# A freshly searched order for all engines, a stricter rule for the last product, and 88 in place of 64 opening identity products, in a fused attention and feed-forward kernel

## The chip, the cores and the metric

The kernel runs on one core of one Trainium2 chip. A core has a matrix engine (TensorE, PE in the profile), a vector engine (VectorE, DVE), an activation engine (ScalarE, ACT), a general engine (GpSimd, POOL) and a synchronisation engine (SyncE, SP) that here issues most of the DMA transfers. Each engine works through its own queue in the order in which the program gave it the instructions. The metric is device time in microseconds (us), the median over runs. Six runs of the kernel before gave 435.27 to 436.93 us, median 435.7.

## The reference

Attention with normalised queries and keys, followed by a two-layer product with a gate between. All matrices are float32 at the boundary.

```python
q, k, v: (8, 12, 448, 64)      # batch, heads, sequence, head width
q_n = q / (norm(q) + 1e-06);  k_n = k / (norm(k) + 1e-06)
scores = q_n @ k_n.T / tau                       # tau = 0.1
attn = softmax(scores)                           # with 1e-09 in the denominator
x = (attn @ v), heads side by side               # (3584, 768)
h = x @ w_in                                     # w_in (768, 2048)
g = h * sigmoid(1.702 * h)
out = g @ w_out                                  # w_out (2048, 768)
```

## The kernel before, in words

**Tiles and names.** The heads are handled in 24 quads `y` of four heads, three quads to a batch element, so that quads 0 to 2 are batch 0, 12 to 14 batch 4, and so on. A quad has two pairs `x` of heads. For each quad these operations exist; the line in brackets is the one under which the profile shows them.

- `load`: q and k (L268 for quad 0, in halves of which SP's and ACT's queue take one each, L276 for the others) and v (L287) come in by DMA. All but ACT's two halves take turns in a fixed sequence.
- `sq` (L309, L310): q and k are squared, 128 x 896 numbers at a time. `red` (L318) sums the squares on DVE.
- the inverse norms: for batch 0 by logarithm, exponential and reciprocal (`root`, `inv`, L330 to L341), later by steps of an iteration on DVE (`norm`, L349 to L377).
- `scale` (L409 for k, in three pieces; L410 for q): multiplication by the inverse norm, into 16 bit.
- `tp`, `qkT` (L434, L445): quads 0 to 4 are transposed on TensorE and copied; later ones by a transposing DMA.
- `kL` (L461): a small copy of the last 64 keys.
- `s` (L483, L512): score products into PSUM; `exp` (L521): the exponential on ACT, which frees the score buffer. There are two score buffers.
- `cast` (L421, L425, L426): v into 16 bit. `at` (L550, L561): the attention product. `nx` (L573, L589): division by the row sum on DVE. `turn`, `x` (L599 to L632): the transposition of the result.

Then follows the feed-forward part. `mm1` (L643, and in halves for batch 0 L674) multiplies by w_in; `th` (L653) is the tanh on ACT and `g` (L660, L686) the gate on DVE; `mm2` (L699) multiplies by w_out in four parts of four products each; `ost` (L712 on DVE, L713 on ACT) copies half a tile of the output out of PSUM, and `st` (L718) stores it. The work of later quads lies beside the feed-forward work of earlier ones.

**The order.** Every operation is added to a plan with an engine, an estimated duration, a due time, its predecessors and the buffers that it takes and frees. While the program is built, `order` plays this through: whenever an engine is free, it takes the ready operation with the earliest due time. The result is the fixed sequence of instructions in each engine's queue; on the chip nothing is rearranged. `tune` first moves each due time by the letter that belongs to it in the string DUES (steps of 0.25 us, the letter K for no move) and chooses an engine for each of 254 operations that have a choice, by the digit in the string ENGINES (0 for the engine given first, 1 and 2 for the alternatives). The turns of the loads are numbered by the due times as they were before the letters are applied. The strings were found by a search outside of the program.

**Identity products.** Ahead of the whole plan, at L989, TensorE multiplies the identity by itself WARM_UP times; nobody uses the result. In the first 48 us of the plan, further identity products (L474) fill gaps that the plan foresees on TensorE; their number follows from the length of the gap.

**The last product's predecessors.** `mm2` of part p reads the gated tiles 4p to 4p + 3. The plan names the gate of the last of these four (for batch 0, whose gates handle two tiles at a time, that of tiles 4p + 2 and 4p + 3) as its predecessor.

Of the kernel before, what the change touches and what calls it, by code (L numbers as in the profile page):

```python
# [24 lines left out]
DMA_ENGINES = 16  # L25
PACKET_US = {256: 0.033, 1024: 0.072, 1536: 0.064, 1792: 0.078, 3072: 0.135, 4096: 0.178}
MOE_FROM, MOE_LAG = 8, 9
FILL_TO, WARM_UP, FILL_US = 48, 64, 0.032
STEPS = "#$%&()*+,-./0123456789:;<=>?@ABCDEFGHIJKLMNOPQRSTUVWXYZ[]^_abcdefghijklmnopqrst"
DUES = (  # L30
    "tGmtOMKLKKMLTPUKXIKtBKATDQKOUH;K:LK#?K>L@]M8MKCE2e>MIKKbHg;BCJKFkIhKKTBLLUKRKrLMFJ]PAK;cgKYKHjpTqCKKXSNt"
    "MKWgSFgKbtNiIT]C7K3KK5ZLtKGQKTcEGPKbFKJ/KtGetI7KAPKLLE?KCK#&@HNM%KMKKLEZk<JJW=KbTKKK@AEPKItMYKtWtETDsG9H"
    "fKSdCWssJLKRRK:KcGK[LHHGGXHt>JAKKcFtJBOOoNKPPMVa_MHN)ttsKTK@KLK@IKaKTiKKCOCInKoYKJKNHnLKRtCBKMLtth[tLtKK"
    "WtttSsJtZPLRKJLHKLKNJKJIKDtKbM@ttQKfWLe@JtGMK;JtKt9KHRKKtKcSL#nsPPmiIqEptsYqKUtS=TMaG]1K1nLrs9[t(tLKeKn["
    "NLSKKVK?KKKtHnf]#[@XMKLBJKc[ICt^3TQ-LN6JHL?<Ka#DtC)KKKIKO(SLPT+IKHSK>KKH#LCKU<KS@HKEI]?KW#GLKK?pLKWKmt3K"
    "tKLK,IJKIKHFL(eGdJZKYRMEFQJCAPOtQM#K/hMKNdNNJ2LLEKPKKKNLKmJKN_T<KOs<t#GHODR?9LU;KOKMT2M9f4KN2#n*1sKT&LKK"
    "Z3<KII3JKJPtKLIKGQStEG@cJsJ3tVKKKKEFtj9.MINAEKJH<KH@KQOE9KJIJ1JAGNHKGG:k$<K)OSBK#LKKRHFL?PLhKgKKfpX004;K"
    "6:tKhKkIK[tNHEKk8L1-KKSWPQI1B1@-L$FQ%dDK#Hp42K;NK(KJFI@&BKUXKKMPRMKG#0%##C1#_K-0JGZYhK#KLcNK8dfKM#J9HpKa"
    "NGJ#Z54KKG)&-PJCF(@KGI7#KCNIG#MkLC<KJKJGV.10oKI7J#M[jM#9LJGIOKKbCMtKK]I]K8ESILPPKG#1&W%UK,JJHQU,+FMKKBJT"
    "MH#K-YhRGd1KJHGEKMPKUGW_aMVKKO=er8JWRLNB@KKASG=Kf=AKUHp^KYHkX=QLJJRiJ>Kbs^UiKKKWIOK637KK$H=*KPKKMJKJP.4F"  # L40
    "KD<RDKD6KK/KD3$J=AH*6G?=G4aF*.K:[KBLLJR+HH#OtHPJ@LLFME@8LVKIN#JKDS)N#UhKL#JNLK*HIBKO;KHt1HTDRKD2@UE7KKMK"
    "MM&K9DIILC:?F?FK&:BWJ?HD]LbLK$5BCN/EY-L#QUMZJHMQ6KLMNJICGFEGO#BKNeohKTKVKGTBK3KLKLJ0ASONK7LL@OA3JKNVKKSO"
    "IRtNOKHOEIKJOXQHIENKJJtQO9K5S,MJSFTBORO@$QKE1DBLKI/HKKSFOKOKISHOKLJFgNDbHKKPNEKL[>PDLKBSDKnKK[2ZLKNTtKsQ"
    "K]IEKVKY*KDKUKUNPJaOb_:SK7ZUMU=tOKHKK3#PJI;o_LK][MKLKKCI/HJa@K#;W+KK-tMXKKLtdG%KIqJEDTYRL,EhKJrKMQ5%HI[P"
    "K#JMHWpNGDPSMINFB^ONJ_&K#K>#iaMj[RJMVLWKOEL_1KCHRTKKRPLFG*#KWPG%LICtI+@FKE9KKBPBK?K?W1=YFKKSMKQWK#?fIsMn"
    "F[JF##KM.JK,4X#KPH)NDIQKQW67AK*KWFLV0EN5ORHM;KIJ/#PKBGQOJK0KPKHU[K+KFKKKQJMJ#Iec3b#KI;7LOH[KK6#KKD4OLBGK"
    "ftKttL"
)
ENGINES = (
    "00200100100101020000000011110010100000111020100110100001110101120000001112000002010000001010100110000211"  # L50
    "10100010100101000000010000000100001000220000001000100000100220100000000000210111010001122101001000000010"
    "0000100000010110100000100001100011000110100010"
)


def packets(n, nbytes):

    one = PACKET_US[nbytes]
    return n * one / DMA_ENGINES, one
# [132 lines left out]
def kernel(  # L192
# [12 lines left out]
    B, H, S, D = q.shape  # L205
    NTOK, DM = out.shape
    DFF = moe_w_in.shape[1]
    P = 112
    C = S // 64
    HP = H // 2  # L210
# [536 lines left out]
    def due_of(y):  # L747
        return 2 * y if y < ND else 4 * y
# [12 lines left out]
    for y in range(NDUO):  # L761
        b, s, grp = y // ND, due_of(y), group_of[y]
# [3 lines left out]
        for ti, nm in ((1, "k"), (0, "q")):  # L766
            pl = on_pool(y, ti)
            n = 0.55 if y == 0 else 1
            for j in (0, 1) if y == 0 else (None,):
# [4 lines left out]
                else:  # L774
# [25 lines left out]
        for ti in (1, 0):  # L800
# [3 lines left out]
                after=[scales[ti]] + [("scale", 1, y)] * (not ti and y > 1), takes=[("qks", 2 if y < 2 else 4 * ti)],  # L804
# [5 lines left out]
        for g in range(2):  # L810
            x = 2 * y + g
            add(("cast", x), "POOL", 1.0, s + (g if first else 2 * g) - 0.5, partial(cast_v, x),
                after=[("load", "v", y, half) for half in range(2)] + [("cast", x - 1)] * g + [("at", x - NV, 1)] * (x >= NV),
                takes=[("vt", 1)], frees=[("v", g)], alts=[("DVE", 0.86)])
        if y < TURNED:
            for ti in (1, 0):
                add(("tp", ti, y), "PE", 0.45, s - 3, partial(turn_qk, y, ti),
                    after=[("scale", ti, y)] + [("tp", 1, y)] * (not ti and y > 1), takes=[("mm", 1), ("qkT", ti)], frees=[("qks", 2)])
# [5 lines left out]
        else:  # L824
            add(("qkT", y), "SP", 3.6, s - 3, partial(dma_turn, y),
                after=[("scale", 0, y), ("scale", 1, y)], takes=[("qkT", 1)], frees=[("qks", 4)],
# [26 lines left out]
        for g in range(2):  # L853
            x = 2 * y + g
            for h in range(2):
# [3 lines left out]
                else:  # L859
# [7 lines left out]
                    after=[("at", x, h)] + [("nx", 2 * y, 0)] * (not turned and g + h > 0) + [("nx", x, 0)] * (whole and h),  # L867
# [21 lines left out]
    def product(name, us, emit, after, takes, frees, tail):  # L889
        moe.append((name, us, emit, after, takes, frees, tail))  # L890

    for b in range(B):
        b2 = b // 2
        units = [(h, m) for h in range(2) for m in range(0, KT2, 2)] if b == 0 else [(b, m) for m in range(KT2)]
        prev = last1
        for u in units:
            key = u if b else u + ("h",)
            m, half = u[1], not b
            after = [prev] if prev else []
            if half and m == 0:  # L900
                after += [("x", x, u[0]) for x in range(HP)]
            elif m == 0:
                after += [("x", x, h) for x in range(b * HP, (b + 1) * HP) for h in range(2) if h and (x < 2 * TX or x % 2)]
            if b == 0:
                after += [("w_in", m // 8, j) for j in range(2)]
            last = u == units[-1]
            prev = ("mm1",) + key
            product(prev, 1.134, partial(mm1_h if half else mm1, *u), after, [("mm", 1)], [("x", HP * last)],
                [("th", "ACT", 0.55, partial(tanh, *key), [("th", 1)], []),
                 ("g", "DVE", 0.62, partial(gate_h if half else gate, *u),  # L910
                  [("g", int(b % 2 == 0 and u == units[0]))], [("th", 1), ("mm", 1)])])
        last1 = prev
        tiles = (0, 1, 2) if b % 2 == 0 else (3, 4, 5, 6)
        for t in tiles:
            for n in range(2):
                for part in range(4):
                    if b:
                        after = [("g", b, 4 * part + 3)]
                    else:
                        after = [("g", h, 4 * part + 2, "h") for h in range(1 + (t > 0))]  # L920
                    after.append(("w_out", part // 2))
                    after += [last2] if last2 else []
                    last2 = ("mm2", b2, t, n, part)
                    last = t == tiles[-1] and n == 1 and part == 3
                    tail = []
                    if part == 3:
                        split = b == B - 1 and t == tiles[-1]
                        tail = [("ost", "ACT", 0.5, partial(halve, b2, t, n), [("ost", 1 - n)], [("mm", 1)])]
                        if n == 1 or split:
                            cols = slice(NW * n, NW * (n + 1)) if split else slice(0, DM)  # L930
                            for i in range(2):
                                queue = "ACT" if split and i else "SP"
                                tail.append((("st", i), queue, packets(64, 4 * (cols.stop - cols.start)),
                                    partial(store, b2, t, i, cols, nc.scalar if queue == "ACT" else nc.sync), i,
                                    [("ost", int(n == 1 and i == 1))]))
                    product(("mm2", b2, t, n, part), 0.652, partial(mm2, b2, t, n, part), after,
                        [("mm", int(part == 0))], [("g", int(last and b % 2))], tail)

    total, done = sum(u[1] for u in moe), 0.0
    for name, us, emit, after, takes, frees, tail in moe:  # L940
        b, part = divmod(B * done / total, 1)
# [82 lines left out]
```

## Time and profile before

| what | value |
|---|---|
| median of six runs | 435.7 us (435.27 to 436.93) |
| the profiled execution, its own time | 437.96 us |
| the profiled execution, span from first to last instruction | 436.2 us |
| mean granted TensorE clock | 0.992 |
| chain that ended last, by engine | PE 80%, DMA 10%, ACT 3%, DVE 3%, POOL 2% |
| exponentials, L521 on ACT | 171, mean 904 ns, 147.5 us busy |
| L699 on PE | 896 products, 157.1 us busy |
| L643 on PE | 672 products, 136.6 us busy |
| opening products, L989 | 64, 5.8 us busy |
| fill products, L474 | 229, 5.8 + 2.8 us busy |

A row of the profile's groups gives the line, the engine, the operation, what it writes and reads with shapes, and a count; then the busy time and the mean of one in ns; then the idle time of the engine just before them, with what ended it. Busy shares of the engines are averages over stages, and a wait matters only where it holds up the chain that ends last. The clock row gives TensorE's granted clock in tenths of full speed over 40 slices. In a list of windows each engine has its busy time and, in brackets, its count of instructions, in the sequence PE, weight loads, DVE, ACT, POOL; then come the granted clock, the DMA share and GB/s. In a timeline a line starts with the start and the duration in us, and ends, in square brackets, with the engine's idle time before and what ended it.

### The profile page before, as it was taken

How to read it: one execution, taken by the hardware profiler on the slowest of the kernel's cores; microseconds unless marked ns; L12 is line 12 of the kernel's file. 1: busy time of each engine (PE TensorE's matmuls, PEld its weight loads, DVE VectorE, ACT ScalarE, POOL GpSimd, SP SyncE). 2: the span in 40 equal slices, each digit the busy share in tenths (PEclk: the TensorE clock that was granted, in tenths of full speed). 3: DMA queues.
4: the chain of work that ended last, by engine and by line, in shares of the span. 5: the costliest groups of instructions: out<-in, count | busy, mean ns of one | idle time of the engine just before them, and what ended most of it. 6: DMA issues, size and time to landing. Idle time of an engine off the chain costs nothing.

```text
span 436.2 us, 9761 instructions
## 1 busy us (share of the span) xinstructions
PE 416.8 (96%) x3893; PEld 254.7 (58%) x3893; DVE 265.1 (61%) x650; ACT 263.1 (60%) x393; POOL 140.0 (32%) x241
## 2 busy tenths in 40 slices
PE   6788999999999799999999999999999999999996
PEld 6667887654566435566455555556546565555563
DVE  5876887689688478756677548785634125525300
ACT  4689884868755968745866557752675654314210
POOL 4965460652223214651455163523130000000000
PEclk9999999999999889999999999999999999999999
DMA  8999799999659997669775976976505214011122
GB/s 284 249 206 234 134 207 229 287 242 253 150 142 221 207 208 163 148 133 245 151 165 121 237 161 176 200 92 112 106 1 91 68 38 80 0 38 36 34 76 72
DMA packets 86541, 65.38 MB, mean 150 GB/s; under 512 B 54624, under 2 KB 81504, under 8 KB 86496
## 3 DMA queue, kind: packets, MB, share of 16 engines
q1 hardware_dynamic: 82304, 57.82, 59.6%
q0 software_dynamic: 3744, 6.29, 8.1%
q8 instruction: 30, 0.49, 0.5%
q10 hardware_dynamic: 448, 0.66, 0.4%
q14 instruction: 15, 0.12, 0.1%
HBM read 47.19 MB, written 11.01 MB: 133 GB/s over the span
## 4 chain that ended last, share of the span: by engine, by line
PE 80%; DMA 10%; ACT 3%; DVE 3%; POOL 2%; issue 1%; SPq 1%; ACTq 0%; POOLq 0%
PE mm L699 32%; PE mm L643 27%; DMA qk<-in_q_dram 10%; PE mm L561 7%; PE sp L483 6%; PE mm L674 4%; PE mm L550 2%; PE sp L512 2%; ACT sq L310 1%; DVE n L318 1%; ACT exp L521 1%; POOL qks L409 1%; SPq L276 0%; ACT ost L713 0%; POOL sq L309 0%
## 5 line engine op out<-in xcount | busy, mean ns | idle before, releaser
L521 ACT ACTIVATE exp<-sp 128x896 f16<-128x896 f32 (+1 forms) x171 | 147.5, 904 | 42.8 <-PE sp L483 39.1
L699 PE MATMUL mm<-w_out,gT 128*128 128x384 f16 x896 | 157.1, 326 | 0.0
L643 PE MATMUL mm<-xT,w_in 128*128 128x448 f16 x672 | 136.6, 355 | 0.1
L699 PEld LDWEIGHTS <-gT 128*128 128x128 f16 x896 | 83.8, 98 | 61.5 <-issue 8.5
L653 ACT ACTIVATE th<-mm 128x448 f16<-128x448 f32 x128 | 69.3, 547 | 63.9 <-PE mm L643 57.6
L643 PEld LDWEIGHTS <-w_in 128*128 128x128 f16 x672 | 64.0, 98 | 63.6 <-issue 7.4
L660 DVE SCALAR_TENSOR_TENSOR gT<-th,mm 128x448 f16<-128x448 f16 x112 | 67.9, 617 | 51.3 <-ACT th L653 49.8
L318 DVE TENSOR_REDUCE n<-sq 128x14 f32<-128x896 f32 (+1 forms) x50 | 51.7, 1042 | 19.8 <-ACT sq L310 16.1
L561 PE MATMUL mm<-vt,exp 128*128 128x65 f16 (+1 forms) x1152 | 56.5, 195 | 0.0
L561 PEld LDWEIGHTS <-exp 128*128 128x128 f16 (+1 forms) x1152 | 51.9, 100 | 5.3 <-issue 2.3
L421 POOL CAST vt<-v 128x384 f16<-128x384 f32 x34 | 18.7, 550 | 103.2 <-PE mm L561 55.7
L713 ACT ACTIVATE ost<-mm 128x384 f32<-128x384 f32 x40 | 19.7, 492 | 50.0 <-PE mm L699 46.0
L550 PE MATMUL mm<-vt,exp 128*128 128x130 f16 x192 | 42.9, 223 | 2.4 <-DVE xT L626 1.5
L483 PE MATMUL sp<-qkT 64*128 64x448 f16 (+1 forms) x324 | 41.2, 335 | 3.7 <-ACT exp L521 3.4
L589 DVE TENSOR_TENSOR xs<-mm,rc 112x256 f16<-112x256 f32 x96 | 40.7, 424 | 3.4
L573 DVE RECIPROCAL rc<-mm 112x4 f32<-112x4 f32 x96 | 17.0, 177 | 40.9 <-PE mm L561 40.6
L409 POOL TENSOR_TENSOR qks<-qk,y 128x384 f16<-128x384 f32 (+1 forms) x45 | 30.6, 708 | 30.8 <-DVE y L377 13.0
L309 POOL TENSOR_TENSOR sq<-qk 128x896 f32<-128x896 f32 (+1 forms) x16 | 26.2, 1635 | 24.6 <-DMA qk<-in_q_dram 9.2
L712 DVE TENSOR_SCALAR ost<-mm 128x384 f32<-128x384 f32 x16 | 8.9, 556 | 38.5 <-PE mm L699 38.5
L310 ACT ACTIVATE sq<-qk 128x896 f32<-128x896 f32 (+1 forms) x30 | 27.3, 913 | 7.2 <-DMA qk<-in_k_dram 3.9
L410 POOL TENSOR_TENSOR qks<-qk,y 128x896 f16<-128x896 f32 x13 | 22.3, 1712 | 7.5 <-DVE kL L461 6.8
L550 PEld LDWEIGHTS <-exp 128*128 128x128 f16 x192 | 19.1, 99 | 8.8 <-issue 5.4
(64 smaller groups left out, 266.8 us busy)
## 6 DMA issues: line engine op xcount, KB each, us to landing
v<-in_v_dram SPq DMA_DIRECT2D x48, 256.0 KB, 5.0
out_dram<-ost SPq DMA_DIRECT2D x54, 192.0 KB, 2.8
qk<-in_k_dram SPq DMA_DIRECT2D x23, 448.0 KB, 5.0
qk<-in_q_dram SPq DMA_DIRECT2D x23, 448.0 KB, 4.5
w_in<-in_moe_w_in_dram POOLq DMA_DIRECT2D x8, 384.0 KB, 14.9
w_out<-in_moe_w_out_dram POOLq DMA_DIRECT2D x2, 1536.0 KB, 15.0
qkT<-qks SPq DMA_TRANSPOSE x38, 4.5
xT<-xs SPq DMA_TRANSPOSE x18, 3.2
```

Of the source, the lines that this page charges most:

```text
L310: return nc.scalar.activation(out=dst, in_=src, func=AF.Square)
L318: return nc.vector.tensor_reduce(out=n2s[y][:, ti, js], in_=sqs[y, ti][:, js], axis=AX.X, op=ALU.add,)
L409: return tuple(eng.tensor_tensor(out=o, in0=a, in1=b, op=ALU.mult) for o, a, b in places(y))
L483: nc.tensor.matmul(out=sp[:, j, at : at + qn], lhsT=qkT[r, g, 1, 128 * n : 128 * (n + 1)], rhs=qkT[r, g, 0, q0 : q0 + qn], start=True, sto ...
L521: return nc.scalar.activation(out=dst, in_=src, func=AF.Exp, scale=inv_tau, **ekw)
L550: nc.tensor.matmul(out=o, lhsT=e[:, (C - 1) * S + a : (C - 1) * S + a + m], rhs=vt[:, 3].rearrange("p j d -> p (j d)"), start=True, stop=F ...
L561: nc.tensor.matmul(out=o[:, (D + 1) * j : (D + 1) * (j + 1)], lhsT=e[:, at : at + m], rhs=vt[:, n, j], start=False, stop=n == 2, skip_grou ...
L589: return nc.vector.tensor_tensor(out=xs, in0=ps[:, :, :D], in1=r[:, :, None].to_broadcast((P, 4, D)), op=ALU.mult,)
L643: nc.tensor.matmul(out=ps[:, :S], lhsT=w_in_sb[:, kk, 128 * m : 128 * (m + 1)], rhs=xTs[b, kk], start=(kk == 0), stop=(kk == KT1 - 1),)
L653: nc.scalar.activation(out=ths[key], in_=mms[key][:, :S], func=AF.Tanh, scale=0.851)
L660: nc.vector.scalar_tensor_tensor(out=gts[b // 2][:, m, (b % 2) * S : (b % 2 + 1) * S], in0=ths.pop((b, m)), scalar=1.0, in1=mms.pop((b, m) ...
L699: nc.tensor.matmul(out=mms[b2, t, n][:, :NW], lhsT=gts[b2][:, kk, 128 * t : 128 * (t + 1)], rhs=w_out_sb[:, kk, NW * n : NW * (n + 1)], st ...
```

## The change

Three things change. WARM_UP goes from 64 to 88. The strings DUES and ENGINES are replaced; the new ones come from a search that ran three times as long and with one more step. The predecessors of `mm2` become all four gates (for batch 0 both gates of two tiles) in place of the last. No operation is added to the plan or taken from it, and none changes its shape; which engine does it, and where it stands in its engine's queue, do.

```diff
-FILL_TO, WARM_UP, FILL_US = 48, 64, 0.032
+FILL_TO, WARM_UP, FILL_US = 48, 88, 0.032
 STEPS = "#$%&()*+,-./0123456789:;<=>?@ABCDEFGHIJKLMNOPQRSTUVWXYZ[]^_abcdefghijklmnopqrst"
 DUES = (
-    "tGmtOMKLKKMLTPUKXIKtBKATDQKOUH;K:LK#?K>L@]M8MKCE2e>MIKKbHg;BCJKFkIhKKTBLLUKRKrLMFJ]PAK;cgKYKHjpTqCKKXSNt"
...
+    "L]Zj_ZKtWtgIZL]]dHKIFKJRtM6KKOSAL;R7DKKNKAKKKL4IQL?KKMKKNAMKOKITMtMKS#EKKPONKHBhIhEbK;XZkNKKQNUK/KEPKKEt"
...
 ENGINES = (
-    "00200100100101020000000011110010100000111020100110100001110101120000001112000002010000001010100110000211"
-    "10100010100101000000010000000100001000220000001000100000100220100000000000210111010001122101001000000010"
-    "0000100000010110100000100001100011000110100010"
+    "00021100010101000101000001100010000001010200000011012001110101102001100120001000010001020100120000000210"
+    "10021111001001000201101100111100000101200111020100100210000201001011100012011010121101021111101100000011"
+    "0011110110001011000010101110101011101010100010"
 )
...
                     if b:
-                        after = [("g", b, 4 * part + 3)]
+                        after = [("g", b, 4 * part + i) for i in range(4)]
                     else:
-                        after = [("g", h, 4 * part + 2, "h") for h in range(1 + (t > 0))]
+                        after = [("g", h, 4 * part + i, "h") for h in range(1 + (t > 0)) for i in (0, 2)]
```

More of the change, by code (lines that the diff above doesn't have):

```diff
@@ L27 @@
 MOE_FROM, MOE_LAG = 8, 9
-FILL_TO, WARM_UP, FILL_US = 48, 64, 0.032
+FILL_TO, WARM_UP, FILL_US = 48, 88, 0.032
 STEPS = "#$%&()*+,-./0123456789:;<=>?@ABCDEFGHIJKLMNOPQRSTUVWXYZ[]^_abcdefghijklmnopqrst"
 DUES = (
-    "tGmtOMKLKKMLTPUKXIKtBKATDQKOUH;K:LK#?K>L@]M8MKCE2e>MIKKbHg;BCJKFkIhKKTBLLUKRKrLMFJ]PAK;cgKYKHjpTqCKKXSNt"
[L32 to L47, printed above, removed]
@@ new lines @@
+    "L]Zj_ZKtWtgIZL]]dHKIFKJRtM6KKOSAL;R7DKKNKAKKKL4IQL?KKMKKNAMKOKITMtMKS#EKKPONKHBhIhEbK;XZkNKKQNUK/KEPKKEt"
+    "KJAH5KKKKKKNYKgR#tL4D]dN=BNGIQtJhOKLHCK=Egs%E/UFUKJDQ4NK:KKBKKE^bPPGJtKTBEA+4FK^KD41BRK^NLGE_SVLEKSKFKPt"
+    "IRJMKWGtUILRKI;Y/KJKKKKRC8KKKKKJKFNM@FCKMTKNKYSKJ(tKGLAFK9JKJHKJM:KHiVSKRBKK:CHnKV@l^KJNgLKKKLSKmqolSsqT"
+    "_if>NtslUJ=tKtaKt^PtiQE5$SKtKistHDEIgKKnjpK2cdjat;A[KiDVt<LMD#KNb=ISKLMKT]t]GKaKAKKt_XK<Kko9s^XNJtLrb:Kt"
+    "LKht]L8ttKGstCZEtKKcLKcMCKDKKF%KKTOGVme3DV?aSQGKIN?OOKOEM(JHdL/DVtIpKAOKEK]>KKQGjKKVtIKfKB>/U?RLGIKLWKKK"
@@ new lines @@
+    "tXA^KLGNNKKtkHKJjJVgt#DStKKsKbhKFA%,KsOKtpKKirKHKhtKsJtBrt2,XLKKcIMLJZJLgK_JKKCJKNSe@3E8UNDYWKK#UX#S^Nti"
+    "KL9K_CtE:RTKNHOBKStIt5K.L^:%tJSKBKKtKKJ0#LKKpOOKKLKHKlgKDKLKKKVKDKTKKL3Q#hK#J#KKKHebHjKPV#KK3EW9@<#t#9WB"
+    "RWII#TI#BKKJOMHK0JMH@LNZjWKK2CO;HM#BEM8X8pKKK#P/O(8K-KK%YH#WGGKX]QIK51Br<:F7IHY-(KKOTQcKHBKKZZ_aka^SLKK#"
+    "..KM:A4KKTjBMGM<LFEQ5KI#LK<IIEWK@KK?&KK#I#KKYKmK#^+##;&*K4EGKKJ+Q3KQKHGFJ#JMT#)KUC#IG>XKKI@JDJKGHIIHK)OT"
+    "SNKJKtKQUKgCcKY$UKsFYAKGTAKRZKKDVHKN4*E0%DfKI9TQPKNKCJK@>>KKKK%:%^6MKKAPH<;KNKH5KKN1KIkFKt4FD#BFMKKK<#KK"
@@ new lines @@
+    "<N<M^PEXK#VE5KKKKAI.KG#KJKDKUEK:LJUB#K<<KO&&bHNC#NKKK&FK6@0<K#S/Q%LKAL6K3)D,1/)P%U#9?#MK#KM#QM<OPCMM#MPZ"
+    "t;2G#FB4=7KP5@7FKK1KK#K:-9=KtPKd;K8BNL_@D$KK:LKQEL>KKKFF+<KQDsFK0@3fIGGKKbG?KnDBL;KF9KKAKkfLKHMSQKPO[IPL"
+    "R%KK)BjCnK$KKKL#PNJ_GSsFPCXM-NNLEJtKFDHK>mK#KKKL=_ZKeSJKBtj@NQHDfF&VKKNZIdEKKK0ITKDSSF#MKOH3RRKJ;O6K(6R^"
+    "t)DK#KKFKPBOOEBDKCIKoLBKML==PKqSIKOM9JIs?K;IL@(LKKK=KHIGM9YPBWKOBVVKGKKXfLDKKTFDDDte@?EH-EKC##[YFKKOGK0N"
+    "Q#M?[YKTHEQUR.K+@H#HKKF?K%PIK>INKG_UHQ>JV:CNDRVKRJNMIJKLHOKFI5-JFKDKKKGHMEUT>M_QONKK@#KYJTRRSJS($MDKHKIM"
@@ L48 @@
+    "KKK:DCF;=YK(KKNWZK^KKK[RRHFU;HP=KK;KL9$@OKKMQHQFE3MGB#MKF?,OHBW^##V=V56KPPWUETaMKSKHMK*IKBKLNBE@K@GJSKI#"
+    "FtKttL"
 )
 ENGINES = (
-    "00200100100101020000000011110010100000111020100110100001110101120000001112000002010000001010100110000211"
-    "10100010100101000000010000000100001000220000001000100000100220100000000000210111010001122101001000000010"
-    "0000100000010110100000100001100011000110100010"
+    "00021100010101000101000001100010000001010200000011012001110101102001100120001000010001020100120000000210"
```

## The prediction

> **What bounds the kernel now.** I read the page's busy shares first, then TensorE's busy time by stretch, then its waits, then the one place where the granted clock falls.
>
> ```profile
> span 436.2 us, 9761 instructions
> PE 416.8 (96%) x3893; PEld 254.7 (58%) x3893; DVE 265.1 (61%) x650; ACT 263.1 (60%) x393; POOL 140.0 (32%) x241
> ...
> PEclk9999999999999889999999999999999999999999
> ```
>
> TensorE is busy for 416.8 of 436.2 us, so it idles 19.4 us; no other engine is above 61%. By stretch: in 0 to 48 us it is busy 36.8 (11.2 idle, and 5.8 of the busy time is the opening products, 8.6 the fill products of L474); in 48 to 140 us it idles 0.2; in 140 to 164 us 3.1; in 164 to 432 us 0.7; after 432 us the last half tile's copy and store take 4.2. So a new order can win in two places only: the opening, and the 24 us from 140. Everywhere else it can only lose. The PEclk row has its dip there too.
>
> The dip by windows of 2 us (busy us with counts, then granted clock, DMA share, GB/s):
>
> ```profile
> 146.00:148.00 2.00, 0.88 (x10) 0.40 (x10) 0.80 (x1) 2.00 (x4) 1.51 (x4) 1.00 0.87 186
> 148.00:150.00 2.00, 1.45 (x30) 1.04 (x27) 1.47 (x3) 2.00 (x3) 1.05 (x2) 0.77 0.93 296
> 150.00:152.00 2.00, 1.75 (x23) 1.29 (x21) 0.74 (x4) 2.00 (x4) 0.00 (x0) 0.50 0.26 79
> 152.00:154.00 2.00, 2.00 (x17) 1.15 (x15) 1.97 (x5) 0.27 (x1) 0.00 (x0) 0.50 0.94 249
> 154.00:156.00 2.00, 2.00 (x7) 0.86 (x6) 0.70 (x4) 0.77 (x2) 0.92 (x3) 0.53 0.96 234
> ```
>
> ACT (fourth figure) has no free moment from 146 to 152 us. TensorE's timeline shows for what it waits, ACT's timeline what it is given:
>
> ```profile
> 146.68 0.36 PE L483 MATMUL sp<-qkT 64*128 64x448 f16 x2 [1.01 <-ACT exp L521]
> 147.49 0.37 PE L483 MATMUL sp<-qkT 64*128 64x448 f16 x2 [0.44 <-ACT exp L521]
> ...
> 149.52 0.56 PE L483 MATMUL sp<-qkT 64*128 64x448 f16 x2 [0.55 <-ACT exp L521]
> 150.32 0.56 PE L483 MATMUL sp<-qkT 64*128 64x448 f16 x2 [0.25 <-ACT exp L521]
> ```
>
> ```profile
> 144.74 0.94 ACT L310 ACTIVATE sq<-qk 128x896 f32<-128x896 f32 x1
> 145.71 1.73 ACT L521 ACTIVATE exp<-sp 128x896 f16<-128x896 f32 x2
> 147.32 0.50 ACT L713 ACTIVATE ost<-mm 128x384 f32<-128x384 f32 x1
> 147.70 0.96 ACT L310 ACTIVATE sq<-qk 128x896 f32<-128x896 f32 x1
> 148.54 1.74 ACT L521 ACTIVATE exp<-sp 128x896 f16<-128x896 f32 x2
> 150.13 0.52 ACT L713 ACTIVATE ost<-mm 128x384 f32<-128x384 f32 x1
> ```
>
> Two squares and two output copies stand between the exponentials that free the score buffers; four waits sum to 2.25 us. Then the clock halves, and the same work takes longer: a block of the attention product 0.44 for 0.255 us (four of them: +0.75), six products of L643 2.24 for 1.14 (+1.1), a last-key score 0.76 for 0.38, two score pairs 0.56 for 0.36 (+0.4), and some 0.2 in the next L643 run: 2.8 us. The place costs 5.1 us.
>
> [...] The trace has the clock at 0.50 after four short waits in 4 us: I take 5.1. [...]
>
> **The change, part by part.**
>
> *88 for 64 products.* The timeline has the 64 from 1.39 to 7.18 us. By 1 us windows, 12 to 14 are touched in each until 6 us, then 22: the pace doubles at 6 us, which the clock row does not show. At the later pace (1 us over about 19, counted without edges, 0.053) 24 more take 1.3 us and end at 8.5. The first real TensorE work starts at 9.39, when DVE's scaled keys arrive, so the 2.2 us of idle hides them with 0.9 to spare. Without that cover they would cost at most 1.3; if all ran at the slow pace (0.1 each, 2.4 us) they would push the start by 0.2. Below nothing: in the shown execution the fill products after 10.2 us run at 0.032 each, so no clock was lost in the gap; nothing to win. **0**, ends 0 and +0.2.
>
> *The output products wait for all four gates, not the last.* This adds no instruction, and DVE's L660 and L686 run each gate in its queue anyway. It binds only the planner. In the last 24.06 us 148 products of L699 run without a break, so there is no gate to wait for. **0**.
>
> *The engine choices.* Decoding the strings against the order in which the operations are added, 112 of 254 differ. Durations are busy time over operations: a key scaling is three pieces (POOL 30.6 / 15 = 2.04; DVE 9.9 / 6 = 1.65), a query scaling 1.71 or 1.14, a square 0.91 ACT, 1.64 POOL, 1.09 DVE, a cast of v 1.15 POOL, 0.94 DVE, an output copy 0.49 ACT, 0.56 DVE.
> - Scalings on DVE go from 18 to 26 (six more key, two more query): DVE +12.2, POOL -15.7.
> - Casts on DVE 14 to 20: DVE +5.6, POOL -6.9.
> - Output copies on DVE 16 to 27: DVE +6.1, ACT -5.4.
> - Squares ACT 30 to 27, POOL 16 to 17, DVE 4 to 6: ACT -2.7, POOL +1.6, DVE +2.2.
> - The small copies (kL, qkT, x): DVE +2.7, ACT -2.5, POOL -1.3.
>
> Sum: **DVE +28.8, ACT -10.6, POOL -22.2 us**, to about 294, 252 and 118. None reaches TensorE's 417, so by totals this is worth nothing; what counts is where. In the order that the program of before emits, the four operations of ACT's rows above are the key and query squares of quad 13 and the two copies of output tile 6. The new string sends the key square to POOL and both copies to DVE: 0.94 + 0.50 + 0.52 = 1.96 us leave ACT just where TensorE waits 2.25 for it. What is late next is the exponentials themselves, 0.3 us. If so, the waits fall by 1.96 and the clock has no reason to halve: **-4.8**. Ends: -5.1 (all gone), and 0 (the new order puts other work between the same exponentials).
>
> *The rest of the order.* Only 118 of the 1670 due letters are the same, against 101 expected from the letters' frequencies alone: this is a fresh order, not a repair of the old one. The loads keep their sequence, since their turns are sorted before the letters are applied; only what lies between them on SP's queue (transposes, stores) moves.
> - Opening, 0 to 48 us. For quad 0 the key scaling goes from DVE (1.22 us, from 8.78) to POOL, where the query's follows it: 2.04 + 1.69 in a row. In its favour, DVE is free to invert the query norm at once instead of at 9.92, and the key halves now lead on both load queues. Nearest rows: POOL's query scaling ends at 12.13; a POOL chain from about 8.5 ends at 12.2. **0**, ends -3 (a quarter of the 11.2 idle) and +2.5 (as much again as the idle of 40 to 48 us, 2.6).
> - 160 to 300 us, where batches 4 to 6 are prepared. DVE is busy 96.3 of 140 us (69%); these batches' share of the shift is 7.0 + 3.8 + 6.4 = 17.2, to 81%. DVE's queue also holds the gates, behind which TensorE's PSUM buffers wait. The trace of before has one such wait after 48 us, 0.9 us at 163. Ends 0 and +5 (below); near the present row I take two more of that size, **+1.7**.
>
> Sum: -4.8 + 1.7 = **-3.1 us**. Span 436.2 to 433.1; the profiled execution 437.96 to 434.9; the median lies 0.5 below the span, **432.6 us**.
>
> **The rivals.**
> - *One stall for another, no change* (434.8 to 436.6). A fresh order drops its own pile-up of exponentials and other work somewhere. For it: the old order had one of 5.1 us, so such orders arise. Against: ACT has 10.6 us less to do. One of 4.8 us gives 432.6 + 4.8 less the 1.7 in the sum: 435.7.
> - *DVE takes ACT's place, slower.* Place: 160 to 180 and 260 to 280 us, where DVE is at 16.9 and 17.0 of 20 already. Spread evenly the shift adds 2.5 to each and fills them to 97%. From the point at which its work passes the 20 us, gates come late, TensorE idles by the excess, and as at 146 us some 2.25 us in short waits halve the clock for another 2.8. Two such places are +10.1: with the gain of 4.8 kept, 435.7 + 5.3 = 441.0; where only one of the two loses the clock, 2.8 less, 438.2. Between them, **439.6**. Against: TensorE waits for DVE almost nowhere now, and the planner can shift gates ahead of scalings.
> - *A better opening as well*: half or more of the -3, and no toll on DVE: 435.7 - 4.8 - 1.5 = **429.4** or a little less.
>
> **The numbers.** This kernel's runs tell 0.2% (0.9 us) from no change. Forecast (431 to 434.8) 0.40; better opening 0.17; no change 0.13; slower 0.30. So faster 0.57, same 0.13, slower 0.30. The likeliest case alone spans 431 to 434.8. The range reaches from 429.3 to 439.5: below it lies half of the better opening (0.08), above it the worse part of the slower cases (0.12), while those in which one place loses the clock lie inside.
>
> **What would show it.** Right: PEclk without a dip at 140 to 160 us, no wait of L483 for exponentials above 0.4 us there, TensorE idle after 48 us under 3 us in place of 4.1 (tail apart), DVE busy near 294, ACT near 252, POOL near 118. The 88 products end near 8.5 us and the first transpose starts within 0.5 us of 9.4. Wrong: a new dip in the clock, L674 or L643 or the attention products waiting for gates or casts by DVE, or an idle opening above 12 us.

## The result, and the profile after

The changed kernel takes **432.19 us** in the median (429.57 to 434.86) beside 435.84 for the kernel before, measured alternately on the same chip: ratio **0.992**, 95% interval 0.990 to 0.994. A second set of runs of the same changed kernel gave 431.82 beside 436.98, ratio 0.989 (0.986 to 0.992). The forecast was 432.6. The gain is there and its size was right; the way to it was only partly the one predicted.

The page of the changed kernel, with the rows that were shown of before:

```profile
span 432.1 us, 9739 instructions
PE 415.7 (96%) x3878; PEld 252.0 (58%) x3878; DVE 291.6 (67%) x710; ACT 253.8 (59%) x374; POOL 123.3 (29%) x200
...
PEclk9899999999999999999999999999999999999999
```

DVE, ACT and POOL moved about as counted (294, 252 and 118 were forecast). The dip of the clock in the middle is gone; a shallow one stands in the second slice. TensorE's busy time hardly changes, as it should with no matmul of the computation added or removed. So look at where it idles. TensorE alone, by stage: the window, then its length, TensorE's busy time and count, granted clock, DMA share, GB/s. First the kernel before:

```profile
0.00:48.00 48.00, 36.83 (x656) 1.00 1.08 241
48.00:140.00 92.00, 91.79 (x898) 1.00 0.96 205
140.00:170.00 30.00, 26.88 (x249) 0.89 0.85 204
170.00:425.00 255.00, 254.27 (x2058) 1.00 0.52 110
```

Then the changed kernel:

```profile
0.00:48.00 48.00, 40.77 (x673) 0.96 1.04 243
48.00:140.00 92.00, 86.97 (x844) 1.00 0.94 193
140.00:170.00 30.00, 30.00 (x240) 1.00 0.93 203
170.00:425.00 255.00, 255.00 (x2112) 1.00 0.55 114
```

Subtracting busy from length gives the idle time by stage: 11.2, 0.2, 3.1, 0.7 before; 7.2, 5.0, 0, 0 after. The 3.1 us at 140 to 170 us are gone, and so is the last wait at 210 us. But **a new hole of 5.0 us has opened at 48 to 140 us**, where the old order had almost none, and the opening idles 4 us less. Not all of these 4 are gain: some of the opening's busy time is fill products, and in this execution the clock was halved for 3.4 us at 17.8 us. What counts is how much work is left at 48 us: TensorE's busy time from there to the end, less what the halved clock stretches, is 377.1 us before (416.8 - 36.83 - 2.8) and 374.9 after (415.7 - 40.77). The opening gains 2.2 us. It gains them late: at 34 us the work left, counted in the same way, is 388.6 us in both kernels, and the difference comes from 40 to 48 us, where the old order waits 1.53 and 1.03 us for DVE. These rows have every engine; first before, then after:

```profile
40.00:48.00 8.00, 5.44 (x75) 4.86 (x70) 5.89 (x16) 5.82 (x11) 3.53 (x7) 1.00 1.11 209
40.00:48.00 8.00, 7.75 (x98) 6.62 (x97) 6.13 (x19) 7.51 (x12) 1.68 (x1) 1.00 1.06 244
```

| part of the span, us | forecast | profiled executions |
|---|---|---|
| opening, 0 to 48 | 0 | -2.2 |
| 140 to 170: waits (2.25 in the stall, 0.87 for a gate at 163) | -1.96 | -3.1 |
| the stall: clock | -2.8 | -2.8 |
| 48 to 140, new idle | not foreseen | +4.8 |
| from 160, DVE's load | +1.7 | -0.7 |
| sum | -3.1 | -4.0 (spans: 436.2 to 432.1) |

The new hole has two main parts (and 0.78 us at 106 us, for a gate). In a second profile of the changed kernel the hole is 4.8 us, in the profile with 64 opening products 3.6. The largest of TensorE's waits in the changed kernel, with the releaser, then the total, the number of times and the longest:

```profile
PE mm L550 <- DVE xs L589: 2.6, 1, 2.6
```

This is an attention product at 85 us that waits for a buffer which the division (L573, L589) empties. DVE's timeline before it shows why the division is late:

```profile
81.95 0.56 DVE L421 CAST vt<-v 128x384 f16<-128x384 f32 x1 [1.17 <-DMA v<-in_v_dram]
...
86.18 1.08 DVE L318 TENSOR_REDUCE n<-sq 128x14 f32<-128x896 f32 x1
87.18 0.17 DVE L573 RECIPROCAL rc<-mm 112x4 f32<-112x4 f32 x1
87.39 0.42 DVE L589 TENSOR_TENSOR xs<-mm,rc 112x256 f16<-112x256 f32 x1
```

DVE works through its queue in order: the last attention products ahead of the division end on TensorE at 83.99 us, and it starts at 87.18. Ahead of it stand the cast of quad 6's v, which waits 1.17 us for a v that lands late, and behind it two reductions and a norm chain for later quads (82.84 to 87.2). The new strings moved this cast from POOL to DVE, but that isn't what makes the wait. With the old engines in the new sequence (below) the cast is back on POOL, the reductions and the norm chain still stand ahead of the division, the first of them waits 2.30 us for a square on POOL whose q came late, and TensorE waits nearly as long:

```profile
PE mm L557 <- DVE xs L596: 2.2, 1, 2.2
```

At 95 us it is the same pattern on ACT:

```profile
95.99 0.49 ACT L713 ACTIVATE ost<-mm 128x384 f32<-128x384 f32 x1 [2.22 <-DMA out_dram<-ost]
```

An output copy waits 2.22 us for an earlier store to leave its buffer. TensorE's next L643 is released by that copy, 1.56 us late:

```profile
96.53 2.43 PE L643 MATMUL mm<-xT,w_in 128*128 128x448 f16 x12 [1.56 <-ACT ost L713]
```

In both cases the queue's next instruction waits for a transfer (the DMA share is 0.94 over this stage), and the work for which TensorE waits stands behind it. It isn't DVE's larger load by itself: the hole is there with the old engines too, and at 140 to 425 us DVE is busy 181 us in place of 156 and TensorE has no wait.

### The profile page after: what moved, and what is told of

Same layout as the page of the kernel before. It is cut to its first block, busy times and chain, and to the rows that moved or that the text cites. A ratio compares the mean times of both kernels' runs of the same rounds, so it can differ in the third digit from the quotient of the medians.

```text
span 432.1 us, 9739 instructions
## 1 busy us (share of the span) xinstructions
PE 415.7 (96%) x3878; PEld 252.0 (58%) x3878; DVE 291.6 (67%) x710; ACT 253.8 (59%) x374; POOL 123.3 (29%) x200
## 4 chain that ended last, share of the span: by engine, by line
PE 84%; DMA 7%; ACT 3%; DVE 2%; SPq 1%; POOL 0%; issue 0%; POOLq 0%; DVEq 0%; ACTq 0%
PE mm L699 31%; PE mm L643 27%; PE mm L561 8%; PE sp L483 8%; DMA qk<-in_q_dram 5%; PE mm L674 4%; PE mm L550 3%; DMA qk<-in_k_dram 2%; PE sp L512 2%; ACT exp L521 2%; SPq L287 1%; DVE gT L660 1%; DVE qks L409 1%; SPq L276 1%; PE sp L474 1%; PE mm L434 1%
## 5 line engine op out<-in xcount | busy, mean ns | idle before, releaser
L521 ACT ACTIVATE exp<-sp 128x896 f16<-128x896 f32 (+1 forms) x171 | 147.3, 903 | 62.3 <-PE sp L483 54.3
L699 PE MATMUL mm<-w_out,gT 128*128 128x384 f16 x896 | 156.8, 326 | 0.0
L643 PE MATMUL mm<-xT,w_in 128*128 128x448 f16 x672 | 134.4, 353 | 2.3 <-ACT ost L713 1.6
L699 PEld LDWEIGHTS <-gT 128*128 128x128 f16 x896 | 83.7, 98 | 62.1 <-issue 9.6
L643 PEld LDWEIGHTS <-w_in 128*128 128x128 f16 x672 | 64.0, 98 | 64.5 <-issue 7.3
L660 DVE SCALAR_TENSOR_TENSOR gT<-th,mm 128x448 f16<-128x448 f16 x112 | 67.8, 617 | 41.0 <-ACT th L653 40.0
L589 DVE TENSOR_TENSOR xs<-mm,rc 112x256 f16<-112x256 f32 x96 | 40.7, 424 | 3.4 <-PE mm L599 0.2
L483 PE MATMUL sp<-qkT 64*128 64x448 f16 (+1 forms) x324 | 41.4, 335 | 1.1 <-ACT qkT L445 1.1
L309 POOL TENSOR_TENSOR sq<-qk 128x896 f32<-128x896 f32 (+1 forms) x17 | 29.2, 1717 | 35.9 <-DMA qk<-in_k_dram 7.1
L712 DVE TENSOR_SCALAR ost<-mm 128x384 f32<-128x384 f32 x27 | 14.9, 554 | 35.6 <-PE mm L699 35.5
L461 POOL COPY kL<-qkT 64x128 f16<-64x128 f16 x36 | 13.2, 367 | 82.6 <-DVE vt L426 39.5
L713 ACT ACTIVATE ost<-mm 128x384 f32<-128x384 f32 x29 | 14.1, 494 | 37.5 <-PE mm L699 35.1
L573 DVE RECIPROCAL rc<-mm 112x4 f32<-112x4 f32 x96 | 17.0, 177 | 25.0 <-PE mm L561 24.4
L310 ACT ACTIVATE sq<-qk 128x896 f32<-128x896 f32 (+1 forms) x27 | 24.4, 908 | 13.4 <-DMA qk<-in_q_dram 5.6
L409 POOL TENSOR_TENSOR qks<-qk,y 128x384 f16<-128x384 f32 (+1 forms) x27 | 18.7, 721 | 39.3 <-DVE y L377 17.0
L421 POOL CAST vt<-v 128x384 f16<-128x384 f32 x28 | 14.2, 508 | 40.9 <-PE mm L561 18.0
```

The lines of the kernel that those rows point to most:

```text
L309: return engines[eng].tensor_tensor(out=dst, in0=src, in1=src, op=ALU.mult)
L310: return nc.scalar.activation(out=dst, in_=src, func=AF.Square)
L483: nc.tensor.matmul(out=sp[:, j, at : at + qn], lhsT=qkT[r, g, 1, 128 * n : 128 * (n + 1)], rhs=qkT[r, g, 0, q0 : q0 + qn], start=True, sto ...
L521: return nc.scalar.activation(out=dst, in_=src, func=AF.Exp, scale=inv_tau, **ekw)
L589: return nc.vector.tensor_tensor(out=xs, in0=ps[:, :, :D], in1=r[:, :, None].to_broadcast((P, 4, D)), op=ALU.mult,)
L643: nc.tensor.matmul(out=ps[:, :S], lhsT=w_in_sb[:, kk, 128 * m : 128 * (m + 1)], rhs=xTs[b, kk], start=(kk == 0), stop=(kk == KT1 - 1),)
```

## The experiments

Each was timed in alternation with the kernel before. They come in four groups: the opening products alone, local repairs at the predicted stall, repairs at other waits, and the sequence taken apart from the engine choices. "Before plus" means the kernel before with one edit.

### The opening products

*Before plus 88 products.*

```diff
-FILL_TO, WARM_UP, FILL_US = 48, 64, 0.032
+FILL_TO, WARM_UP, FILL_US = 48, 88, 0.032
```

> The kernel before with 88 in place of 64 opening products and nothing else. My theory: they lie in TensorE's 2.2 us of idle before the first transpose, so the time is that of before within 0.4 us, the opening products end near 8.5 us, and the first transpose starts at 9.4. Rival 1: they push the first transpose back, +0.2 to +1.3 us. Rival 2: they keep the clock up in the opening in some executions, -0.5 to -2 us and a higher mean clock.

Measured 437.38 beside 435.88, ratio 1.003 (1.001 to 1.004): a little slower. The timeline shows that the first transpose was not held up:

```profile
9.32 0.23 PE L434 MATMUL mm<-ident,qks 128*128 128x128 f16 x1 [0.32 <-DVE qks L409]
```

The products end at 9.00 and it starts at 9.32 (9.39 in the kernel before). So "costs nothing" holds for the start of the first transpose, and yet the runs are 0.27% slower; where these 1.2 us go isn't visible in one profile and stays open. That two programs can differ by as much whatever their products do was not ruled out. The same profile has a second finding. The four waits of the predicted stall are all there, some 1.6 us later:

```profile
148.32 0.36 PE L483 MATMUL sp<-qkT 64*128 64x448 f16 x2 [1.01 <-ACT exp L521]
...
151.15 0.37 PE L483 MATMUL sp<-qkT 64*128 64x448 f16 x2 [0.55 <-ACT exp L521]
151.96 0.36 PE L483 MATMUL sp<-qkT 64*128 64x448 f16 x2 [0.44 <-ACT exp L521]
```

And the clock stays at 1.00 behind them (TensorE by windows of 2 us):

```profile
150.00:152.00 2.00, 1.01 (x22) 1.00 1.22 269
152.00:154.00 2.00, 2.00 (x34) 1.00 1.04 339
```

In the kernel before, the clock was halved from 149.07 us on, amid the same waits, for 6.8 us. So these waits do not bring the halving by themselves. It is no rare thing here either: of the eight profiles of the old sequence with its own engines, edits included, four have a stretch that begins at 149 to 152 us (one of 6.8 us, three of 3.4; the mean clock from 140 to 170 us is 0.89 in the first and 0.93 to 0.94 in the others) and four have none there.

*Before plus 40 products* (40 in the same line).

> The kernel before with 40 opening products. Theory A (every opening product costs its 0.05 us, since the longer kernels measured about 1.2 us more for 24 products): the time falls by 1.2 us to 434.7. Theory B (what counts is how TensorE's clock comes up, and 64 are near enough): with 40 the clock is half in the opening in more executions, the mean granted clock falls below 0.994, and the time is 436.5 to 438. Theory C (the difference between 64 and 88 was the spread between programs, not the products): within 0.7 us of 435.8.

Measured 437.49 beside 435.48, 1.004 (1.003 to 1.006). TensorE then idles 3.83 us ahead of the first transpose, and the clock is halved from 9.5 to 12.9 us: six transposes at 10.13 us take 0.82 us (0.51 in the kernel before), the 56 fill products behind them 2.77 (1.80).

*The changed kernel with 64 products.*

> The changed kernel with 64 opening products, all else as changed. My theory: within 0.4 us of the changed kernel (432.2), the dip of the clock near 18 us neither better nor worse. Rival: the new order starts its first transpose a microsecond sooner and needs the longer warm-up: without it the clock dips earlier or longer, +0.5 to +2 us.

Measured 431.38 beside 435.88, 0.988 (0.986 to 0.991), against 0.992 and 0.989 with 88: no difference can be told, though six runs would not show one of 0.27%. The whole gain is there without the added products.

### Local repairs at the predicted stall

*Before plus the three operations moved off ACT.* The sequence stays; the key square of quad 13 goes to POOL, the two output copies to DVE.

```diff
+    SWITCH = {('sq', 1, 13): 'POOL', ('ost', 0, 6, 0): 'DVE', ('ost', 0, 6, 1): 'DVE'}
...
+        for name, eng in self.SWITCH.items():
+            self.ops[name] = (eng, *self.ops[name][1:])
```

> The kernel before, its order kept, with only three operations moved to another engine at the same place in the order: the key square of quad 13 from ACT to POOL, the two output copies of tile 6 from ACT to DVE. My theory: TensorE's waits for exponentials at 146 to 151 us fall from 2.25 to about 0.3 us, the clock keeps 1.0 there, and the time falls by 4 to 5 us to about 431. Rival 1 (the waits end but the clock falls for another reason): -2 us, 433.8. Rival 2 (the exponentials alone hold TensorE up, or DVE and POOL are late instead): 0, 435.8.

Measured 436.08 beside 435.88, 1.001 (1.000 to 1.003): no gain. The waits barely move (the lines added shift L483 to L497, L521 to L535):

```profile
145.74 0.36 PE L497 MATMUL sp<-qkT 64*128 64x448 f16 x2 [1.07 <-ACT exp L535]
146.55 0.36 PE L497 MATMUL sp<-qkT 64*128 64x448 f16 x2 [0.44 <-ACT exp L535]
```

Two more, of 0.17 and 0.44, follow at 148 and 149 us. In sum that is 2.12 in place of 2.25 (2.44 in the kernel with 88 products, where the clock was full), and the wait for a gate that was 0.87 us at 163 us is 2.30 here. ACT's own timeline shows what became of the time freed on it: it turned into waiting.

```profile
144.77 1.73 ACT L535 ACTIVATE exp<-sp 128x896 f16<-128x896 f32 x2 [0.93 <-PE sp L497]
```

ACT now waits 0.93 us for scores. So the step that carried -4.8 in the prediction falls. With two score buffers, score products and exponentials take turns. In the old sequence they are packed here with little other TensorE work between; in the new one 12 products of L699 and more stand there:

```profile
144.78 1.30 PE L699 MATMUL mm<-w_out,gT 128*128 128x384 f16 x7
146.01 0.55 PE L483 MATMUL sp<-qkT 64*128 64x448 f16 x4
146.50 2.12 PE L699 MATMUL mm<-w_out,gT 128*128 128x384 f16 x12
```

That this taking of turns sets the waits would fit both; it isn't shown, since the edit that pulls the scores of the old order apart (below) took only 0.24 us off them.

*Before plus identity products in those gaps.* Products that nobody uses fill the waits, so that TensorE doesn't go idle.

```diff
+    def pad(corner, n):
+        for _ in range(n):
...
+            if y == 10 and g == 1 and n > 0:
+                pad(mms[0, 6, 1][:, NW : NW + 64], 31 if n == 1 else 13)
...
+        if (x, h) == (20, 1):
+            pad(ps[:, 264:328], 25)
```

> The kernel before, its order kept, with 69 more identity products on TensorE (44 beside the two pairs of scores of quad 10 that wait, 25 behind the attention product that follows), 2.2 us in all at 32 ns each, so that TensorE is busy while it waits for the exponentials at 146 to 150 us. The waits themselves stay. My theory (short idle gaps close together let the clock fall): the clock keeps 1.0 from 148 to 156 us and the time falls by about 2.8 us to 433.0. Rival (the clock falls for another reason[...]): no change, 435.8, or +0.5 where the products come in the way.

Measured 437.73 beside 435.88, 1.003 (1.001 to 1.005). At 148 to 156 us the clock stays at 1.00, with one wait of 0.33 us left, and nothing is gained. The profiled execution has its half-clock stretches at 43 and 166 us instead, and over the runs the mean granted clock is 0.993 beside 0.995, so it did not rise. Either the dip at this place is worth less than 2.8 us in an average run, or the products cost elsewhere what they save here.

*Before plus the scores of quad 10 earlier.* The sequence is edited: the score products and their exponentials are moved behind other work, as below.

```diff
+    MOVES = [(('exp', 8, 1, 2), ('s', 10, 0), ('exp', 10, 0, 1), ('exp', 10, 0, 0)), (('at', 17, 1), ('s', 10, 'l'), ('exp', 10, 'l')), (('mm2', 0, 6, 1, 1), ('s', 10, 1), ('exp', 10, 1, 0), ('exp', 10, 0, 2))]
```

(The first name of each group is what the others are placed behind.)

> The kernel before with one stretch of its order changed, engines as they were: three steps of quad 10's scores and their exponentials move up by two to four parts of L699 each, so that products of L699 stand between one pair of scores and the next. My theory now: TensorE waits at 146 to 150 us because its own queue has nothing but scores there while two score buffers go back and forth between it and ACT; with other products between, the 2.25 us of waits shrink by 1.5 us or more, and the time falls by as much, to 434.4 or less. Rival (the stage is held by late loads, and what is won comes back as a longer wait for gates near 160 us): the waits shrink, the wait of L550 for a gate grows from 0.9 to 2 us or more, and the time stays within 0.7 us of 435.8.

Measured 436.81 beside 435.48, 1.001 (0.999 to 1.004). The waits are now 0.18, 1.39 and 0.44, in sum 2.01: pulled apart in one place and closed up in the next.

### Repairs at other waits

*The same with the norm work of quads 13 and 14 later*, to bring forward the gate at 163 us for which TensorE waits 0.9 us.

```diff
+    MOVES = [... (('nx', 18, 0), ('red', 0, 14), ('norm', 0, (13, 14)), ('norm', 1, (13, 14)))]
```

(The dots stand for the three groups above.)

> The same, and in addition DVE takes the last reduction and the norm steps of quads 13 and 14 after the gates and the division that TensorE waits for near 160 us, not ahead of them. My theory: both waits go, the time falls by 2.5 to 3.5 us to about 432.8, near the changed kernel without its other stages. Rival (TensorE's idle in this stage is set by the arrival of the data of batch 2 and 4, whatever the order): within 0.7 us of the kernel with the first edit alone.

Measured 441.55 beside 435.48, 1.012 (1.007 to 1.017): clearly slower. TensorE's timeline (L643 is L657 here, L660 is L674):

```profile
163.89 0.22 PE L564 MATMUL mm<-vt,exp 128*128 128x130 f16 x1 [0.80 <-DVE gT L674]
169.77 2.40 PE L657 MATMUL mm<-xT,w_in 128*128 128x448 f16 x6 [3.10 <-DVE gT L674]
```

The first wait is as it was. The norm chain that was put back runs on DVE from 166.5 to 169.1, ahead of the next gate (169.11), and a wait of 3.10 us is new. A wait of 0.9 was attacked and one three times as long made.

*Before plus the reductions and norms of quad 4 later*, against the waits of 1.53 and 1.03 us at 40 and 46 us.

```diff
+    MOVES = [(('nx', 4, 1), ('red', 1, 4)), (('g', 0, 4, 'h'), ('red', 0, 4), ('norm', 0, (4,)))]
```

> The kernel before, engines as they were, with the two reductions of quad 4 (and its norm steps) moved behind the copies, divisions and gates of batch 0 on DVE, behind which TensorE waits 1.53 us at 40 and 1.03 us at 45 us. My theory: the opening's gain of the changed kernel (some 2 us by 48 us) is that no such reduction, whose keys come late, stands ahead of them: the two waits fall below 0.5 us each and the time by 1.5 to 2.5 us, to about 433.8. Rival (the opening is held by the loads and comes out even later on): waits fall, time within 0.7 us of 435.8.

Measured 435.98 beside 435.48, 1.001 (0.998 to 1.004). Waits of 2.56 us in sum became 0.76 at 42 us and 0.72 at 50 us, and the time didn't follow.

*The changed kernel, 64 products, with the division put first at 85 us.* Against the 2.58 us wait shown above (1.11 us in the profile with 64 products), the norm steps and scalings of quad 6 and one reduction of quad 7 are placed behind the operation `x` of pair 10.

```diff
+    MOVES = [(('x', 10, 1), ('norm', 0, (6,)), ('norm', 1, (6,)), ('red', 1, 7), ('scale', 1, 6), ('scale', 0, 6))]
```

> The changed kernel with 64 products, and with the divisions of quad 5 and one copy ahead of quad 6's norm steps and one reduction in DVE's order, since TensorE waits 2.6 us (1.1 us with 64) for these divisions at 85 us. If waits add up along TensorE, it is 1 to 2.5 us faster than the kernel with 64 alone (0.988): 0.983 to 0.986. If, as with the edits of the old order, a wait that is taken away comes back behind the work that was put later, 0.987 to 0.990 or worse.

Measured 431.64 beside 436.98, 0.991 (0.988 to 0.994); the unedited changed kernel in the same comparison had 0.989. The wait is gone, so what stood ahead of the division in DVE's queue had made it. The next two waits are 1.74 us at 94 us, for a copy on ACT (1.72 without the edit, for another copy), and one at 99.7 us for a gate, where the unedited order waits 0.60:

```profile
99.72 2.28 PE L657 MATMUL mm<-xT,w_in 128*128 128x448 f16 x6 [2.02 <-DVE gT L674]
```

### Sequence and engine choices taken apart

Each string was replaced alone. The sequence is worked out with a kernel's own pair of strings; then every operation that has a choice is put on the engine that the other kernel's string names, without moving it.

```diff
+        for (name, choices), c in zip(self.alts.items(), self.OTHER):
+            self.ops[name] = (choices[int(c)][0], *self.ops[name][1:])
```

*The changed kernel with the old engines* (and its 88 products).

> The changed kernel's order (and its 88 products), but each of the 112 operations that changed engine back on its old one, at its place in the order. Theory A (the gain is in the sequence, above all TensorE's own, which keeps it fed where the old one had nothing for it; the engines are not near their limits): within 1.5 us of the changed kernel, 431 to 434. Theory B (the engine choices carry it: ACT's 10.6 us less): it loses the gain, 435.8 or more. Theory C (choices and sequence are tuned to each other and neither works alone): slower than before, 438 or more.

Measured 436.44 beside 436.98, 0.998 (0.996 to 0.9995).

*The kernel before with the new engines* (and its 64 products).

> The counterpart: the order of the kernel before with the changed kernel's engine choices. Theory A (sequence): no gain, 435.5 to 437.5. Theory B (engines): 431 to 434. Theory C (tuned to each other): 438 or more.

Measured 444.22 beside 436.98, 1.017 (1.014 to 1.020).

*The changed kernel again*, in the same comparison.

> The changed kernel once more, beside the others of this call. If 88 products cost what they cost in the old order (0.27%), it stands 0.2 to 0.4% above the same kernel with 64, which measured 0.988 of before: 0.991 to 0.993. If the two differ by nothing, 0.988 to 0.990. Its second profile shows which of its idle times (85, 95, 106 us) come back and whether the clock dips at 18 us again.

Measured 431.82, 0.989 (0.986 to 0.992). So the new sequence alone brings -0.24%, the new engines alone cost +1.69%, and together they bring -1.1%. TensorE by stage, first the new sequence with the old engines:

```profile
0.00:48.00 48.00, 38.95 (x664) 1.00 1.04 246
48.00:140.00 92.00, 87.40 (x847) 1.00 0.93 191
140.00:170.00 30.00, 29.99 (x241) 1.00 0.94 207
```

then the changed kernel again (its other stages are as in its first profile):

```profile
0.00:48.00 48.00, 41.68 (x690) 1.00 1.03 247
```

and the old sequence with the new engines:

```profile
140.00:170.00 30.00, 24.30 (x256) 0.97 1.02 221
```

Read the third row of the first list: **the new sequence alone removes the stall** at 140 to 170 us (29.99 of 30), with ACT as loaded as before. The new engines in the old sequence leave it: at 150 to 153 us TensorE waits 1.07, 0.44, 0.17 and 0.44 for exponentials, the very figures that the three moved operations left, and a wait of 2.42 for a gate comes on top:

```profile
150.07 0.36 PE L490 MATMUL sp<-qkT 64*128 64x448 f16 x2 [1.07 <-ACT exp L528]
...
166.90 0.22 PE L557 MATMUL mm<-vt,exp 128*128 128x130 f16 x1 [2.42 <-DVE gT L667]
```

The second row of the first list shows that the new hole at 48 to 140 us also belongs to the sequence. The engine choices pay in the first stage: with them the opening has 2.7 us more of busy TensorE, of 4.2 us between the two spans (434.2 and 430.0). The first difference is at the transpose of quad 0's query, for which the old engines have TensorE wait until 12.75 us:

```profile
12.75 0.56 PE L441 MATMUL mm<-ident,qks 128*128 128x128 f16 x7 [2.43 <-POOL qks L417]
```

With the new ones it starts at 12.03, after 1.57 us, and the first scores follow at 14.16 in place of 15.67 (12.07 and 15.31 in the first profile). Which of the choices in the opening is worth how much was not tried singly.

## Why the prediction was right, and where it was not

**88 products, cost 0.** The time of the work itself was right: in the changed kernel they run from 1.38 to 7.78 us (8.5 was the estimate) and the first transpose starts at 8.39, a microsecond earlier than before, not later. The cover has become thin: in the second profile of the changed kernel the first transpose follows the products without a gap, at 8.02 us. The total for the change fits as well, since 64 and 88 can't be told apart in it. But in the old order the same edit costs 0.27%, outside the ends given as 0 and +0.2 us, and 40 products cost 0.44%. The reason given for "nothing to win" was also too firm: it said that the gap before the first transpose loses no clock. In the profile of the kernel with three operations moved, that gap is 2.18 us and the clock is halved right behind it, from 9.3 us on (the mean from 9 to 13 us is 0.57). In two more profiles of the old sequence with 64 products, those of quad 10's scores moved up and of quad 4's reductions put later, the mean clock of the first 48 us is 0.93 and the products run at full pace from 36 us on, so clock was lost ahead of that there too.

**The output products wait for all gates, cost 0.** Right. The sequence that `order` works out under the old rule and under the new one is the same for each pair of strings.

**The engine counts.** Right within 6 us: DVE +26.5, ACT -9.3, POOL -16.7 against +28.8, -10.6, -22.2. That the choices count by where they fall and not by their totals held; but the place was the opening and not the stall.

**The stall at 146 us, -4.8.** Here the prediction was near in the sum (between the two profiled executions 5.1 us went from this place) and wrong twice in the reason. First, it is not the three operations on ACT: moved alone they took 0.13 us off the waits, since ACT stood waiting for scores. The step saw that ACT had no free moment and concluded that less on ACT means earlier exponentials; that holds only if the scores are there. What removed the stall is the new sequence. Second, the clock half, -2.8. The stretch at half speed was real in that execution, but it does not follow from the waits (the kernel with 88 products has the same ones without it), and other profiles have such stretches at 10 us (three operations moved), at 43 and 166 us (identity products in the gaps) and at 100 us (the division put first) as well as at 150. The mean granted clock over the runs is 0.993 to 0.995 before and 0.995 to 0.996 after. Within one comparison the new order has 0.08% (with 64 products) or 0.21% (with 88) more of it, which is 0.3 to 0.9 us over the whole kernel, in place of 2.8. In runs with a mean clock of 0.997 or more, where next to none was lost, the kernel before has medians of 434.8 to 436.3 us and the changed one of 431.1 to 431.6: the gain of some 4 us is nearly all idle time.

The row from which the 5.1 us were taken was read rightly in that the clock was lost amid waits of at most 1.01 us; but it fell at 149.07 us, after two of the four waits and not after all, and it was priced wrongly. Half of 6.8 and three times 3.4 us, spread over the eight profiles of the old sequence with its own engines, is 1.1 us each: an estimate from so few, but with it the place was worth some 3.3 us and not 5.1.

**The opening, 0 with ends -3 and +2.5.** The mis-sized term: -2.2 in the first profile, and -4.2 in the second, counted in the same way. For the chain that the prediction compared, it was nearly right: quad 0's query is transposed from 12.07 and 12.03 us on beside 12.19 in the kernel before, and the first scores come later than there (15.31 and 14.16 beside 13.99). What the new engines save there against the old ones only makes good what the new sequence alone would lose. The gain over the kernel before comes further on: the work left at 34 us is 388.6 us before and 388.6 and 386.6 after, and from 40 to 48 us TensorE idles 2.56 us before and 0.25 and 0.35 after. The prediction looked no further than quad 0. What this idle is worth alone stays open: the edit that shortened these waits in the old order (quad 4 later) brought no time. The rival "a better opening as well" had the right stage and rightly no toll on DVE.

**DVE's load from 160 us, +1.7.** It did not come. TensorE has not one wait of note after 140 us. The rival in which DVE takes ACT's place fails with it: the windows it named are full.

**One stall for another.** This rival was right as a mechanism: the new order does bring a hole, +4.8 us, of just the size of the one removed (4.8 was the figure used). Its cause is not a pile-up of exponentials but work behind late transfers. The sign that was to show the forecast right, idle below 3 us after 48 us in place of 4.1, failed: it is 5.0. Signs of being wrong came too: a dip of the clock, at 17.8 us, and L643 and the attention products waiting for DVE. So it was luck that the median came out right. Errors of both signs cancel: a stall priced with more clock than the runs lose and a new hole of 4.8 us that was not foreseen, against an opening that gained where 0 was put and a toll of 1.7 us on DVE that did not come.

## What to carry to other kernels

Where every engine works through a fixed queue, a wait in the profile marks a place in the sequence, not a cost that can be taken off by itself: five edits here went against chosen waits of 0.9 to 2.6 us, a sixth took 2 us of work off the engine that was waited for, and none gained anything that could be measured; in most of them a wait came back at the next place where the order was tight. Ask of an engine that looks full whether it would have its inputs earlier, before counting work taken from it as time won; sequence and engine choices had to be changed together here, since each alone gave -0.24% and +1.69% where both gave -1.1%. And price a dip of the clock by the mean clock over many runs, never by the one execution that was profiled.

## What the runs showed of the hardware

**Stretches at half clock have no fixed place.** In the first profile of the kernel before, the clock is halved from 149.07 us on, for 6.83 us; in that of the changed kernel from 17.82 us on, for 3.41 us. In both it is halved once more behind the last product, from 435.79 and from 430.83 us on. The recorded stretches at full speed ahead of and between these are 143.36 and 279.89 us long before, 13.65 and 409.60 us after. These four and the two halved ones ahead of the last product are whole multiples of 3.413 us, so that within each of the two executions the changes lie on one grid; no run here sets where it begins. Nor does the length of the waits tell whether the clock falls: it was lost amid waits of 1.01, 0.44 and 0.55 us close together in one execution (the kernel before) and not with the same three in another (with 88 products), and after a single gap of 2.18 us at the opening in one (three operations moved) and not after 2.22 us in another (the kernel before). What decides it was not shown.

**Filling gaps with idle products bought nothing.** With products in the waits the granted clock stayed at 1.00 from 148 to 156 us of the profiled execution, the mean clock over the runs was 0.993 beside 0.995, and the time rose by 0.28%.
